# Logit sums in four 32-column groups of TensorE, with the softmax in (slot, head) by token, in a four-layer attention and state-space kernel

## Chip, cores and metric

The kernel runs on one core of a Trainium2 chip. The metric is the device time of one execution in microseconds (us), the median of several runs. Engines: PE is TensorE (PEld its weight loads), DVE is VectorE, ACT is ScalarE, POOL is GpSimd, SP is SyncE, whose queue issues the DMAs. PSUM is the memory that PE writes.

## Reference

The input x is 2048 tokens by 512 features, bfloat16. Four layers follow, A, B, A, B, each of them `x = x + layer(layernorm(x))`, with the same weights in both A and in both B. Layer A, which the change touches, is attention over a dilated window:

```python
H = 32; Dh = D // H            # 32 heads of 16
W, dil = 8, 2                  # 8 keys per token: itself and those 2, 4, ... 14 tokens before
idx = pos[:, None] - off[None, :]
mask = idx >= 0
logits = jnp.einsum("bhsd,bhswd->bhsw", q, kg) * scale
logits = jnp.where(mask[None, None, :, :], logits, -1e9)
attn = _softmax(logits, axis=-1)
o = jnp.einsum("bhsw,bhswd->bhsd", attn, vg)
```

q, k and v come from `x @ wqkv`, and `o @ wo` is what is added to x. Layer B is a long convolution (a state-space kernel), done as a Fourier transform by matmuls; the change leaves it alone.

## The kernel before

Token t sits at partition t // 16 and slot t % 16, so that a slot is a set of 128 tokens, one per partition. Four slots make a block q; there are four blocks. q and k are held transposed (feature by token; four feature tiles `ft` of 128 features, which is 8 heads each), v as token by feature, for 16 slots and 14 slots before them that hold the same rows moved by one partition (`v_ext`, filled by DMA, lines 356 and 357).

Layer A runs in two stretches, in `core` (line 307). In the first, for each block q and feature tile ft:

- `mult` (line 295, DVE) multiplies q with the eight shifted k into the tile prod, 128 features by (8 window positions, 4 slots, 128 tokens). prod has two buffers.
- `lsum` (line 302, PE) sums each head's 16 features. prod is the stationary operand, 128x128 for each window position and slot, and the moving operand is `ind8`, an indicator of 8 columns, one for each of the 8 heads. That is 32 matmuls. The result L (128 tokens by (slot, window, head), float32) fills two PSUM banks; L has two buffers.
- After the last ft, `mask` (line 285, PE) adds -1e9 on partition 0 for positions before the first token.

In the slots of the next block follow `mx` (line 365, DVE maximum over the window), `sub_exp` (line 372, PE subtracts the maximum from L by a matmul with the negative identity; line 375, ACT exponential into ex), `recip` (line 382, PE sums over the window; lines 384 and 386, ACT logarithm and exponential for the reciprocal rs) and `norm_p` (line 392, DVE, attn = ex times rs). Between these stand the projections `q_proj` (line 185) and `v_proj` (line 351) on PE, evacuated by ACT (lines 187 and 353) from two PSUM buffers pq.

In the second stretch, for each slot n in the order 0, 2, 1, 3, 4 ... 15: `pv_mult` (line 402, DVE) multiplies attn with the eight shifted v into pav (two buffers), `pv_sum` (line 412, PE) sums over the window and transposes into po (one buffer), ACT copies it to oT (line 415), and `out_proj` (lines 422 and 424, PE) of the slot before adds x and the projection; ACT writes x back (lines 428 and 430) and takes the layer norm sums (line 108). Blocks 2 and 3 of the softmax, and the products and sums of block 3, lie in this stretch too. In layer 0 ACT also computes sine tables there (line 700) and copies the convolution kernel (line 1354).

The order of all this on PE, DVE, ACT and SP is fixed by the order in which the program calls the functions, inside `tc.manual_schedule`; POOL is left to the scheduler. Before, the order came from loops in `core` with conditions on n and a count `per` that spread the projections; work of other layers came in through a table of events `ev`. The first three products of layer 0 and their sums are called earlier, from `k_gen` (ORDERK, letters X and Z), and share `mult` and `lsum`.

Of the kernel before, what the change touches and what calls it, by code (L numbers as in the profile page):

```python
# [20 lines left out]
P = 128  # L21
# [45 lines left out]

def build_a_consts(tc, nc, cpool, tpool):
# [14 lines left out]
    ind8 = cpool.tile([P, 8], BF16, name="ind8")  # L83
    nc.vector.tensor_tensor(ind8[:], m1[:], m2[:], ALU.mult)
    c["ind8"] = ind8
    rows = cpool.tile([1, P], BF16, name="rows")
    nc.vector.memset(rows[:], 0.0)
    nc.vector.memset(rows[:, 0:1], 1.0)
    c["e0"] = rows[:]
    mv = tpool.tile([1, NA, W], I32, name="iota_mask")  # L90
    nc.gpsimd.iota(mv[:], pattern=[[1, NA], [-2, W]], base=0, channel_multiplier=0)
    mrow = cpool.tile([1, NA, W], BF16, name="maskrow")
    nc.vector.tensor_scalar(mrow[:], mv[:], 0, -1e9, ALU.is_lt, ALU.mult)
    c["maskrow"] = mrow
    c["zrow"] = rows[:, 64:128]
# [67 lines left out]
class LayerA:  # L163
# [110 lines left out]
    def linit(self, q):  # L274
        if "L" in self.st[q]:
            return
        self.st[q]["L"] = self.ps_l.tile([P, 4, W, H], F32, name="L")

    def mask(self, q):
        L = self.st[q]["L"]  # L280
        for j in range(2):
            a = q * 4 + 2 * j
            w0 = a // 2 + 1
            if w0 < W:
                self.nc.tensor.matmul(L[:, 2 * j:2 * j + 2, w0:], lhsT=self.c["e0"],
                                      rhs=self.c["maskrow"][:, a:a + 2, w0:].unsqueeze(3).to_broadcast([1, 2, W - w0, H]),
                                      start=False, stop=True, skip_group_check=True)
# [10 lines left out]
    def lsum(self, q, ft):  # L298
        pr, L = self.st[q].pop(ft), self.st[q]["L"]
        for w in range(W):  # L300
            for al in range(4):
                self.nc.tensor.matmul(L[:, al, w, ft * 8:(ft + 1) * 8], lhsT=pr[:, w, al, :], rhs=self.c["ind8"][:],  # L302
                                      start=(ft == 0 and w == 0 and al % 2 == 0), stop=True, skip_group_check=True)
        if ft == NDT - 1:
            self.mask(q)

    def core(self, x_sb, u, lnp, ev=None, nprod=0):
# [5 lines left out]
        ev = ev or {}  # L313
# [3 lines left out]

        def event(key):
            for f in ev.get(key, ()):
                f()  # L320

        with ExitStack() as c2:
# [25 lines left out]
            def v_proj(a):  # L348
# [5 lines left out]
                if a >= 14:  # L354
# [5 lines left out]
                    event(("v", b))  # L360

            def mx(q):
                L = st[q]["L"]
                m = wk.tile([P, 4, H], BF16, name="mx", bufs=1)
                nc.vector.tensor_reduce(m[:], L[:].rearrange("p a w h -> p a h w"), AX.X, ALU.max)
                st[q]["mx"] = m

            def sub_exp(q):
                L, m = st[q]["L"], st[q]["mx"]
                ex = wk.tile([P, 4, W, H], BF16, name="ex", bufs=1)  # L370
                for j in range(2):
                    nc.tensor.matmul(L[:, 2 * j:2 * j + 2], lhsT=nident[:],
                                     rhs=m[:, 2 * j:2 * j + 2].unsqueeze(2).to_broadcast([P, 2, W, H]),
# [4 lines left out]
            def recip(q):  # L378
                ex, L = st[q]["ex"], st[q]["L"]
                tot = L[:, 0, 0:4, :]  # L380
                for w in range(W):
                    nc.tensor.matmul(tot, lhsT=ident[:], rhs=ex[:, :, w, :], start=(w == 0), stop=(w == W - 1), skip_group_check=True)
                ssum = wk.tile([P, 4, 1, H], F32, name="ssum")
                nc.scalar.activation(ssum[:, :, 0, :], tot, ACT.Ln)
                rs = wk.tile([P, 4, 1, H], BF16, name="rs", bufs=1)
# [3 lines left out]
            def norm_p(q):  # L389
                ex, rs = st[q]["ex"], st[q]["rs"]  # L390
                attn = wk.tile([P, 4, W, H], BF16, name="attn", bufs=2)
                nc.vector.tensor_tensor(attn[:], ex[:], rs[:].to_broadcast([P, 4, W, H]), ALU.mult)
# [4 lines left out]
            def pv_mult(n):  # L397
# [4 lines left out]
                nc.vector.tensor_tensor(pv[:], attn[:, n % 4].unsqueeze(2).to_broadcast([P, W, DH, H]), vap, ALU.mult)  # L402
# [57 lines left out]
            projs = [(q_proj, 1, ft) for ft in range(NDT)] if 1 not in self.qT else []  # L460
            vs = [*range(0, NA, 2), *range(1, NA, 2)]
            projs += [(v_proj, a) for a in vs[:6]] + [(q_proj, 2, ft) for ft in range(NDT)]
            projs += [(v_proj, a) for a in vs[6:]]
            slots = [(0, ft) for ft in range(nprod, NDT)] + [(q, ft) for q in (1, 2) for ft in range(NDT)]
            free = 2 if l else 0
            lead = 0 if l else 2
            per, acc = (len(projs) - lead) / (len(slots) - free - 0.5), float(lead)

            def proj(n):
                nonlocal acc  # L470
                acc += n
                while acc >= 1 and projs:
                    f, *args = projs.pop(0)
                    f(*args)
                    acc -= 1

            for q, ft in slots:
                if q == 1 and ft == 0 and 1 not in self.qT:
                    while 1 not in self.qT or projs[0][0] is q_proj:
# [1000 lines left out]
```

## Time and profile before

| | us |
|---|---|
| median of 3 runs | 422.05 |
| lowest, highest | 421.33, 422.5 |
| the profiled execution, its own time | 418.89 |
| its span in the profile | 417.1 |

In that execution layer 0's logits and projections run from about 104 to 140 us, its weighted sums over v from 140 to 196; in layer 1 from 276 to 312 and from 312 to 364.

| group | count | mean ns |
|---|---|---|
| line 402 DVE products with v | 32 | 2283 |
| line 295 DVE products q with k | 29 + 3 | 2299, 2281 |
| line 302 PE logit sums, 128x8 | 928 + 96 | 166 each, pipelined |
| line 285 PE mask | 14 | 197 to 358 |
| line 365 DVE maximum | 8 | 1218 |
| line 375 ACT exponential | 8 | 1026 |
| line 392 DVE normalization | 8 | 693 |

Timeline rows give start, duration, engine, line, operation, output and input tile with shapes; a number in brackets is the time for which the engine sat idle before the row, with the instruction that ended the wait. A stretch's row gives from:to, its length, and for each engine the busy time with the count of instructions. Matmuls overlap, so that a matmul's duration is its latency, and the spacing of starts is what a stream costs.

### The profile page before, as it was taken

How to read it: one execution, taken by the hardware profiler on the slowest of the kernel's cores; microseconds unless marked ns; L12 is line 12 of the kernel's file. 1: busy time of each engine (PE TensorE's matmuls, PEld its weight loads, DVE VectorE, ACT ScalarE, POOL GpSimd, SP SyncE). 2: the span in 40 equal slices, each digit the busy share in tenths (PEclk: the TensorE clock that was granted, in tenths of full speed). 3: DMA queues.
4: the chain of work that ended last, by engine and by line, in shares of the span. 5: the costliest groups of instructions: out<-in, count | busy, mean ns of one | idle time of the engine just before them, and what ended most of it. 6: DMA issues, size and time to landing. Idle time of an engine off the chain costs nothing.

```text
span 417.1 us, 15864 instructions
## 1 busy us (share of the span) xinstructions
PE 320.5 (77%) x7048; PEld 231.5 (55%) x7106; DVE 387.9 (93%) x515; ACT 321.7 (77%) x552; POOL 37.7 (9%) x46
## 2 busy tenths in 40 slices
PE   3000068999999987778998779999998978896885
PEld 2000036667756565556887768555665655566774
DVE  8999999999899999996999969979779999989995
ACT  6999998987445569987999998863555758779972
POOL 3000200000396000000500000000000020000000
PEclk9999998999999999999999999999999999999899
DMA  8940642113014666393226597730043027504506
GB/s 222 383 125 13 73 90 71 33 40 89 14 40 123 179 180 189 99 389 109 70 89 229 217 306 218 231 99 2 3 114 89 5 79 328 156 3 140 168 10 197
DMA packets 62462, 54.36 MB, mean 130 GB/s; under 512 B 33877, under 2 KB 50874, under 8 KB 61114
## 3 DMA queue, kind: packets, MB, share of 16 engines
q1 hardware_dynamic: 62250, 53.22, 42.0%
q8 instruction: 55, 0.90, 0.9%
q10 hardware_dynamic: 144, 0.13, 0.1%
q14 instruction: 13, 0.11, 0.1%
HBM read 30.28 MB, written 13.24 MB: 104 GB/s over the span
## 4 chain that ended last, share of the span: by engine, by line
PE 35%; DVE 21%; ACT 14%; issue 5%; DMA 5%; SPq 3%; DVEq 0%; ACTq 0%
PE pq L351 6%; DVE pav L402 5%; DVE t L805 5%; PE L L302 4%; DVE a1s L745 4%; PE pk L1175 4%; PE pq L185 3%; DVE prod L295 3%; PE pp L242 3%; PE po L412 3%; PE pp L1113 3%; PE pq L424 2%; SPq L1280 2%; DMA w_sb<-w_dram 2%; ACT ub L818 1%
## 5 line engine op out<-in xcount | busy, mean ns | idle before, releaser
L402 DVE TENSOR_TENSOR pav<-attn,v_ext 128x4096 bf16<-128x4096 bf16 x32 | 72.8, 2283 | 0.1
L295 DVE TENSOR_TENSOR prod<-qT,kT_ext 128x4096 bf16<-128x4096 bf16 x29 | 66.0, 2299 | 3.9 <-PE L L302 3.8
L412 PE MATMUL po<-ident,pav 64*128 64x64 bf16 x2048 | 36.3, 190 | 15.1 <-DVE pav L402 7.7
L412 PEld LDWEIGHTS <-pav 64*128 64x128 bf16 x2048 | 32.5, 95 | 26.0 <-DVE pav L402 14.9
L1103 PE MATMUL pt<-ident,x_blk 128*128 128x128 bf16 x64 | 7.0, 260 | 43.4 <-ACT x_blk L158 43.4
L1015 DVE TENSOR_TENSOR A_t<-A_t,pow_t 128x1024 bf16<-128x1024 bf16 (+4 forms) x46 | 38.1, 868 | 0.2
L424 PE MATMUL pq<-wop,oT 128*128 128x512 bf16 x121 | 31.7, 379 | 4.3 <-issue 3.8
L353 ACT CAST v_ext<-pq 128x512 bf16<-128x512 f32 x32 | 18.8, 587 | 19.2 <-PE pq L351 17.5
L818 ACT CAST ub<-pb 128x1024 bf16<-128x1024 f32 x32 | 32.2, 1036 | 1.7 <-DVE t L805 0.8
L763 PE MATMUL pb<-a1s,w_sb 128*128 128x64 bf16 x768 | 28.4, 196 | 6.2 <-ACT a1s L745 2.9
L302 PEld LDWEIGHTS <-prod 128*128 128x128 bf16 x928 | 27.0, 96 | 8.1 <-DVE prod L295 2.5
L1103 PEld LDWEIGHTS <-x_blk 128*128 128x128 bf16 x64 | 5.4, 117 | 46.1 <-ACT x_blk L158 44.4
L745 DVE CAST a1s<-pb 128x1024 bf16<-128x1024 f32 x23 | 27.0, 1215 | 3.9 <-PE pb L756 3.9
L763 PEld LDWEIGHTS <-w_sb 128*128 128x128 bf16 x768 | 25.8, 100 | 8.6 <-issue 6.8
L351 PE MATMUL pq<-wv,xnT 128*128 128x512 bf16 x118 | 29.9, 379 | 0.5
L1113 PE MATMUL pp<-xnT,kT_ext 128*128 128x512 bf16 x87 | 25.0, 406 | 6.2 <-ACT qT L1118 3.3
L302 PE MATMUL L<-ind,prod 128*128 128x8 bf16 x928 | 27.4, 166 | 0.8 <-DVE prod L295 0.6
L415 ACT CAST oT<-po 128x512 bf16<-128x512 f32 x32 | 18.5, 577 | 11.5 <-PE po L412 11.2
L745 ACT CAST a1s<-pb 128x1024 bf16<-128x1024 f32 x25 | 24.9, 1034 | 2.5 <-PE pb L756 2.2
L1175 PEld LDWEIGHTS <-A_t 128*64 128x64 bf16 (+1 forms) x512 | 22.3, 105 | 3.6
L1175 PE MATMUL pk<-B_t,A_t 128*64 128x84 bf16 (+1 forms) x512 | 24.1, 203 | 0.1
L832 PE MATMUL pb<-Wp,t 64*128 64x64 bf16 x512 | 19.4, 192 | 5.9 <-ACT ub L818 2.8
(225 smaller groups left out, 809.8 us busy)
## 6 DMA issues: line engine op xcount, KB each, us to landing
w_sb<-w_dram SPq DMA_DIRECT2D x8, 1024.0 KB, 9.4
w_dram<-w_zero SPq DMA_DIRECT2D x1, 4096.0 KB, 14.8
kf_ring<-kf_dram SPq DMA_DIRECT2D x13, 256.0 KB, 3.7
kf_ring<-kf_dram SPq DMA_DIRECT2D x26, 128.0 KB, 3.6
v_ext<-v_ext SPq DMA_DIRECT2D x4, 784.0 KB, 6.2
x_blk<-in_A_x_dram SPq DMA_DIRECT2D x4, 512.0 KB, 4.1
kT_ext<-in_A_wqkv_dram SPq DMA_DIRECT2D x4, 512.0 KB, 10.1
x_sb<-in_A_x_dram SPq DMA_DIRECT2D x4, 512.0 KB, 5.4
```

The costliest lines, as they stand in the source:

```text
L295: nc.vector.tensor_tensor(pr, self.qT[q][:, ft].unsqueeze(1).to_broadcast([P, W, 4, P]), kap, ALU.mult)
L302: self.nc.tensor.matmul(L[:, al, w, ft * 8:(ft + 1) * 8], lhsT=pr[:, w, al, :], rhs=self.c["ind8"][:], start=(ft == 0 and w == 0 and al % ...
L351: nc.tensor.matmul(pp[:], lhsT=xnT[:, dt, a * P:(a + 1) * P], rhs=wv[:, dt, :], start=(dt == 0), stop=(dt == NDT - 1))
L402: nc.vector.tensor_tensor(pv[:], attn[:, n % 4].unsqueeze(2).to_broadcast([P, W, DH, H]), vap, ALU.mult)
L412: nc.tensor.matmul(po[:, h, 0, ft, :], lhsT=pvf[rows, w, ft * P:(ft + 1) * P], rhs=ident[rows, rows], start=(w == 0 and ft == 0), stop=(w ...
L424: nc.tensor.matmul(pw[:], lhsT=oT[:, ftp, :], rhs=self.wo[:, ftp, :], start=False, stop=(ftp == NDT - 1))
L745: (self.nc.scalar.copy if eng == "act" else self.nc.vector.tensor_copy)(dst, src)
L763: nc.tensor.matmul(p2[:, j, :], lhsT=self.w2[:, ec * EC + j, :], rhs=a1s[:, ec * EC + j, :], start=True, stop=True)
L818: nc.scalar.copy(ub[:], p2)
L1015: return lambda: nc.vector.tensor_tensor(*args)
L1113: nc.tensor.matmul(pps[kind, b, ft][:], lhsT=la.wqk[:, dt, c:c + P], rhs=la.xnT[:, dt, b * 512:(b + 1) * 512], start=(dt == 0), stop=(dt = ...
L1175: nc.tensor.matmul(o, lhsT=lhs, rhs=Bt[:, ri, c * CH + ql].rearrange("p b g -> p (b g)"), start=(not half and j % 4 == 0 and ri == 0), sto ...
```

## The change

The roles of the two matmul operands in `lsum` are exchanged. The indicator, now 32 columns wide (one of the four feature tiles' 8 heads filled, the rest zero), is the stationary operand; the products are the moving one, 512 columns at a time (4 window positions by 128 tokens). The four slots of a block go to PSUM partitions 0, 32, 64 and 96. That is 8 matmuls per lsum, and L becomes (slot, head) by (window, token). All four feature tiles add into the same 32 partitions of a slot.

The mask becomes a matmul of 4 rows that picks the slot, and touches token column 0 alone. Maximum, subtraction, exponential, sum and reciprocal do the same in the new layout, without a change of size; the normalization is done in place, in ex. A new step `turn` follows it: 8 PE transposes of 128x128 (one per window position) into the second bank of L, and one ACT copy from there into attn, which now lies as token by (window, slot, head).

The loops of `core` are replaced by two strings, CORE0 and CORE1, one letter per call. Read letter by letter they give the order that the loops gave, with T (turn) added: after the normalization of blocks 0 and 1 at the end of the last slot of the following block, and right after the normalization of block 2 (fifth product with v) and of block 3 (twelfth).

```diff
+CORE0 = """
+0mvvvvlmvvxlemqqlmqqlrmvvlnTmvvxlvemvlmvvlrmvvlnTqPxSePmqSOl1PrSO2Pm3qSOlPnT4SOPm56qSOl7P8ASOPmb
+BSOlPxdwCSeOPaaDSOPraaSOPnTbSOPd9ESOPaaFGSOPaaHSOPbtStO
+"""
+CORE1 = """
+0m1l2ml3mqqlmqqvlmvvxlvemvvlmqqlrmqqvlnTmvvxlvemvvlmvvlrmvvlnTqPxSePmqSOlPrSOPmqSOlPnTSOPmqSOlPS
+OPmbSOlPxdwSeOPaaSOPraaSOPnTbSOPdSOPaaSOPaaSOPbtStdaaaaO
+"""
+ROWS0 = (0, 2, 1, 3, 4, 5, 6, 7, 8, 9, 10, 11, 12, 13, 14, 15)
+ROWS1 = (0, 2, 1, 3, 4, 5, 6, 7, 8, 9, 10, 11, 12, 13, 14, 15)
+VROWS = (*range(0, 16, 2), *range(1, 16, 2))
...
-    ind8 = cpool.tile([P, 8], BF16, name="ind8")
-    nc.vector.tensor_tensor(ind8[:], m1[:], m2[:], ALU.mult)
-    c["ind8"] = ind8
-    rows = cpool.tile([1, P], BF16, name="rows")
-    nc.vector.memset(rows[:], 0.0)
-    nc.vector.memset(rows[:, 0:1], 1.0)
-    c["e0"] = rows[:]
-    mv = tpool.tile([1, NA, W], I32, name="iota_mask")
-    nc.gpsimd.iota(mv[:], pattern=[[1, NA], [-2, W]], base=0, channel_multiplier=0)
-    mrow = cpool.tile([1, NA, W], BF16, name="maskrow")
-    nc.vector.tensor_scalar(mrow[:], mv[:], 0, -1e9, ALU.is_lt, ALU.mult)
-    c["maskrow"] = mrow
-    c["zrow"] = rows[:, 64:128]
+    ind = cpool.tile([P, NDT * H], BF16, name="ind32")
+    nc.gpsimd.memset(ind[:], 0.0)
+    diag = bass.AP(tensor=ind.tensor, offset=ind[:].offset, ap=[list(ind[:].ap[0]), [H + 8, NDT], [1, 8]])
+    nc.vector.tensor_tensor(diag, m1[:].unsqueeze(1).to_broadcast([P, NDT, 8]), m2[:].unsqueeze(1).to_broadcast([P, NDT, 8]), ALU.mult)
+    c["ind"] = ind[:].rearrange("p (t h) -> p t h", t=NDT)
+    zrow = cpool.tile([1, 64], BF16, name="zrow")
+    nc.gpsimd.memset(zrow[:], 0.0)
+    c["zrow"] = zrow[:]
+    sv = tpool.tile([4, 4, H], I32, name="iota_slot")
+    nc.gpsimd.iota(sv[:], pattern=[[-1, 4], [0, H]], base=0, channel_multiplier=1)
+    slot = cpool.tile([4, 4, H], BF16, name="slot_sel")
+    nc.vector.tensor_scalar(slot[:], sv[:], 0, None, ALU.is_equal)
+    c["slot"] = slot[:].rearrange("k a h -> k (a h)")
+    mv = tpool.tile([4, 4, W], I32, name="iota_mask")
+    nc.gpsimd.iota(mv[:], pattern=[[4, 4], [-2, W]], base=0, channel_multiplier=1)
+    keep = cpool.tile([4, 4, W], BF16, name="slot_mask")
+    nc.vector.tensor_scalar(keep[:], mv[:], 0, -1e9, ALU.is_lt, ALU.mult)
+    c["mask"] = keep
...
-        self.st[q]["L"] = self.ps_l.tile([P, 4, W, H], F32, name="L")
+        self.st[q]["L"] = self.ps_l.tile([P, W, P], F32, name="L")
 
     def mask(self, q):
         L = self.st[q]["L"]
         for j in range(2):
-            a = q * 4 + 2 * j
-            w0 = a // 2 + 1
-            if w0 < W:
-                self.nc.tensor.matmul(L[:, 2 * j:2 * j + 2, w0:], lhsT=self.c["e0"],
-                                      rhs=self.c["maskrow"][:, a:a + 2, w0:].unsqueeze(3).to_broadcast([1, 2, W - w0, H]),
-                                      start=False, stop=True, skip_group_check=True)
+            w0, w1 = max(2 * q + 1, 4 * j), 4 * j + 4
+            if w0 < w1:
+                self.nc.tensor.matmul(L[:, w0:w1, 0], lhsT=self.c["slot"], rhs=self.c["mask"][:, q, w0:w1], start=False, stop=True,
+                                      skip_group_check=True)
 
...
     def lsum(self, q, ft):
         pr, L = self.st[q].pop(ft), self.st[q]["L"]
-        for w in range(W):
+        for j in range(2):
             for al in range(4):
-                self.nc.tensor.matmul(L[:, al, w, ft * 8:(ft + 1) * 8], lhsT=pr[:, w, al, :], rhs=self.c["ind8"][:],
-                                      start=(ft == 0 and w == 0 and al % 2 == 0), stop=True, skip_group_check=True)
+                self.nc.tensor.matmul(L[al * H:(al + 1) * H, 4 * j:4 * j + 4, :], lhsT=self.c["ind"][:, ft, :],
+                                      rhs=pr[:, 4 * j:4 * j + 4, al, :], start=(ft == 0), stop=True, skip_group_check=True)
         if ft == NDT - 1:
             self.mask(q)
 
...
             def mx(q):
                 L = st[q]["L"]
-                m = wk.tile([P, 4, H], BF16, name="mx", bufs=1)
-                nc.vector.tensor_reduce(m[:], L[:].rearrange("p a w h -> p a h w"), AX.X, ALU.max)
+                m = wk.tile([P, P], BF16, name="mx", bufs=1)
+                nc.vector.tensor_reduce(m[:], L[:].rearrange("c w p -> c p w"), AX.X, ALU.max)
                 st[q]["mx"] = m
 
             def sub_exp(q):
                 L, m = st[q]["L"], st[q]["mx"]
-                ex = wk.tile([P, 4, W, H], BF16, name="ex", bufs=1)
+                ex = wk.tile([P, W, P], BF16, name="ex", bufs=1)
                 for j in range(2):
-                    nc.tensor.matmul(L[:, 2 * j:2 * j + 2], lhsT=nident[:],
-                                     rhs=m[:, 2 * j:2 * j + 2].unsqueeze(2).to_broadcast([P, 2, W, H]),
+                    nc.tensor.matmul(L[:, 4 * j:4 * j + 4], lhsT=nident[:], rhs=m[:].unsqueeze(1).to_broadcast([P, 4, P]),
                                      start=False, stop=True, skip_group_check=True)
                 nc.scalar.activation(ex[:], L[:], ACT.Exp, scale=scale)
                 st[q]["ex"] = ex
 
             def recip(q):
-                ex, L = st[q]["ex"], st[q]["L"]
-                tot = L[:, 0, 0:4, :]
+                ex, tot = st[q]["ex"], st[q]["L"][:, 0, :]
                 for w in range(W):
-                    nc.tensor.matmul(tot, lhsT=ident[:], rhs=ex[:, :, w, :], start=(w == 0), stop=(w == W - 1), skip_group_check=True)
-                ssum = wk.tile([P, 4, 1, H], F32, name="ssum")
-                nc.scalar.activation(ssum[:, :, 0, :], tot, ACT.Ln)
-                rs = wk.tile([P, 4, 1, H], BF16, name="rs", bufs=1)
+                    nc.tensor.matmul(tot, lhsT=ident[:], rhs=ex[:, w, :], start=(w == 0), stop=(w == W - 1), skip_group_check=True)
+                ssum = wk.tile([P, P], F32, name="ssum")
+                nc.scalar.activation(ssum[:], tot, ACT.Ln)
+                rs = wk.tile([P, P], BF16, name="rs", bufs=1)
                 nc.scalar.activation(rs[:], ssum[:], ACT.Exp, scale=-1.0)
                 st[q]["rs"] = rs
 
             def norm_p(q):
                 ex, rs = st[q]["ex"], st[q]["rs"]
-                attn = wk.tile([P, 4, W, H], BF16, name="attn", bufs=2)
-                nc.vector.tensor_tensor(attn[:], ex[:], rs[:].to_broadcast([P, 4, W, H]), ALU.mult)
+                nc.vector.tensor_tensor(ex[:], ex[:], rs[:].unsqueeze(1).to_broadcast([P, W, P]), ALU.mult)
+
+            def turn(q):
+                ex = st[q]["ex"]
+                pt = st[q]["L"][:, 4:8, :].rearrange("c w p -> c (w p)").bitcast(BF16).rearrange("p (w c) -> p w c", w=W)
+                for w in range(W):
+                    nc.tensor.transpose(pt[:, w, :], ex[:, w, :], ident[:])
+                attn = wk.tile([P, W, 4, H], BF16, name="attn", bufs=2)
+                nc.scalar.copy(attn[:].rearrange("p w a h -> p w (a h)"), pt)
                 st[q]["attn"] = attn
 
...
-                nc.vector.tensor_tensor(pv[:], attn[:, n % 4].unsqueeze(2).to_broadcast([P, W, DH, H]), vap, ALU.mult)
+                nc.vector.tensor_tensor(pv[:], attn[:, :, n % 4, :].unsqueeze(2).to_broadcast([P, W, DH, H]), vap, ALU.mult)
```

In the driver, each letter calls the next of its kind: m `mult`, l `lsum`, q and v the projections, x `mx`, e `sub_exp`, r `recip`, n `norm_p`, T `turn`, P `pv_mult`, S `pv_sum`, O `out_proj`, t, b, d and a layer norm steps; digits, w and capital A to H stand for what came in by events.

```diff
+            for c in "".join(order.split()):
+                if c in ev:
+                    ev[c]()
+                else:
+                    next(ops[c])()
```

## The prediction, before the result was known

> **What bounds the kernel now.** I read the page's part 1 first, then busy time by stretches around the two attention layers, then the timelines of VectorE (DVE), TensorE (PE) and ScalarE (ACT) there.
>
> ```profile
> PE 320.5 (77%) x7048; PEld 231.5 (55%) x7106; DVE 387.9 (93%) x515; ACT 321.7 (77%) x552; POOL 37.7 (9%) x46
> ```
>
> DVE is the fullest engine, but the change removes nothing from it. So I ask where DVE waits for PE. By stretch (us, then PE, PEld, DVE, ACT busy): logits and projections of layer 0, its weighted sums over v, the same two of layer 1.
>
> ```profile
> 117.00:139.80 22.80, 22.31 (x338) 14.15 (x344) 21.71 (x13) 11.60 (x22) 15.05 (x10) 1.00 0.43 111
> 139.80:196.00 56.20, 45.42 (x1290) 30.86 (x1304) 53.22 (x46) 45.93 (x97) 1.02 (x1) 1.00 0.57 182
> 282.00:312.00 30.00, 29.63 (x402) 17.89 (x406) 24.89 (x14) 15.80 (x29) 0.00 (x0) 1.00 0.16 41
> 312.00:364.00 52.00, 43.12 (x1283) 29.70 (x1299) 51.68 (x42) 36.00 (x86) 2.89 (x1) 1.00 0.38 132
> ```
>
> In layer 1's logits PE is full (29.63 of 30.00) and DVE is not (24.89); layer 0's logits are balanced; both sums over v are DVE's alone. What PE saves counts only as DVE's waits, which stand in brackets on its timeline:
>
> ```profile
> 114.87 4.49 DVE L295 TENSOR_TENSOR prod<-qT,kT_ext 128x4096 bf16<-128x4096 bf16 x2 [2.07 <-PE L L302]
> ...
> 127.89 0.73 DVE L392 TENSOR_TENSOR attn<-ex,rs 128x1024 bf16<-128x1024 bf16 x1 [0.37 <-ACT rs L386]
> ...
> 139.30 0.69 DVE L392 TENSOR_TENSOR attn<-ex,rs 128x1024 bf16<-128x1024 bf16 x1 [0.72 <-ACT rs L386]
> ```
> ```profile
> 294.96 2.29 DVE L295 TENSOR_TENSOR prod<-qT,kT_ext 128x4096 bf16<-128x4096 bf16 x1 [0.87 <-PE L L302]
> 298.55 0.69 DVE L392 TENSOR_TENSOR attn<-ex,rs 128x1024 bf16<-128x1024 bf16 x1 [1.29 <-ACT rs L386]
> ...
> 311.69 0.69 DVE L392 TENSOR_TENSOR attn<-ex,rs 128x1024 bf16<-128x1024 bf16 x1 [1.29 <-ACT rs L386]
> ```
>
> With the rows at 288.47 (0.61), 301.61 (0.17) and 308.11 (0.87) layer 1 has 5.10 us of such waits. From 312 to 363 DVE's rows follow one another without an idle bracket, so whatever stalls DVE there is paid in full.
>
> [...] Here two 64-column groups do run together, in full: line 756's pairs start 5 ns apart and the next pair 55 ns later; four groups no run here shows. [...]
>
> ```profile
> 196.36 0.22 PE L756 MATMUL pb<-F1c,k_perm 128*64 128x128 bf16 x1
> 196.36 0.22 PE L756 MATMUL pb<-F1s,k_perm 128*64 128x128 bf16 x1
> 196.41 0.22 PE L756 MATMUL pb<-F1c,k_perm 128*64 128x128 bf16 x1
> ```
>
> **The logit sums.** One lsum was 32 matmuls of 8 columns at a pitch of 25 ns, 0.80 us (rows 123.26 to 124.06). It becomes 8 matmuls of 512 columns in two rounds of four column groups. A 512-column stream takes 0.215 us (8 of line 185 from 121.53 on), so two rounds are 0.43 if four groups run together, plus about 0.03 of stagger. Each lsum now enters and leaves a column mode:
>
> ```profile
> 195.74 0.38 PE L424 MATMUL pq<-wop,oT 128*128 128x512 bf16 x1
> ...
> 196.05 0.24 PE L756 MATMUL pb<-F1c,k_perm 128*64 128x128 bf16 x1
> ```
>
> 0.31 us from start to start where 0.215 is the stream: 0.095 to enter. Leaving, 210.46 to 210.61 with 0.053 of stream, is also 0.095. Sum 0.43 + 0.03 + 0.19 = 0.65 us: **0.15 us saved** per lsum, not the 0.37 that the matmuls alone promise. Bounds: 0.45 (switches hidden) to 1.91 (no concurrency, 8 x 0.215 + 0.19). The mask matmuls shrink from up to 448 columns to four at most: block 0's lsum with mask took 1.34 us (117.22 to 118.56), so its mask 0.54; block 1's 0.42 (128.76 to 129.98). New: two small matmuls and a further switch, 0.13. Saved 0.41 and 0.29.
>
> **Layer 1, logits.** Up to the reciprocal of block 1, whose result DVE awaits at 311.69, PE runs ten lsums after the first bound one: 10 x 0.15 + 0.41 + 0.29 = 2.20 us less. The turn of block 0 stands in PE's order there: 8 transposes at 55 ns (line 231: 16 in 0.89 us) are 0.44 us more. Its wait for the normalization hides: that is done at 299.24, and PE gets to it after the lsum at 300.29 and its mask. Its ACT copy (1.01 us by the row xnT<-pt of line 233, same shape) fits ACT's gaps, 15.80 busy of 30; behind it wait the casts of the next v rows, for which pq has two buffers. Net 2.20 - 0.44 = **-1.8 us** of the 5.10.
>
> **Layer 0, logits.** Three lsums precede the product at 114.87, which waited 2.07 for the last of them: -0.7, a little over 0.15 each because the array leaves another column mode before two of them anyway and because the last one's end comes sooner. Then the waits of 0.37 and 0.72 go: PE saves four lsums and a mask, 1.01, before the first, and in all eight lsums and two masks less a turn, 1.46, before the second, against 1.09 to be had. **-1.8 us**; more DVE cannot give.
>
> **The turn in the sums over v.** The normalization of blocks 2 and 3 used to be followed on DVE by products that read it directly. For block 2 four products lie between. For block 3 nothing lies between but small statistics:
>
> ```profile
> 351.58 0.68 DVE L392 TENSOR_TENSOR attn<-ex,rs 128x1024 bf16<-128x1024 bf16 x1
> ...
> 352.45 2.29 DVE L402 TENSOR_TENSOR pav<-attn,v_ext 128x4096 bf16<-128x4096 bf16 x1
> ```
> ```profile
> 353.37 0.19 ACT L118 ACTIVATE ln_rstd<-ln_veps 128x4 f32<-128x4 f32 x1
> ```
>
> The product at 352.45 must now wait for 8 transposes (from 352.3 to 352.9, PE being idle) and then for ACT, which is busy without a gap until it issues the row at 353.37. The copy takes that place and ends near 354.4; the product starts at 354.5: **2.05 us** of new DVE stall, with all DVE rows behind it. The lower bound is an ACT that is free, 1.6 us; the upper, an ACT a row later, 2.8. On PE the sum of row 11 queues behind the turn, 0.7 us late, which the stall covers. Of the stall 0.25 comes back at the end: the last sum began at 362.36, 0.3 after its product, because ACT and PE lagged, and a lag is caught up while DVE stands. Layer 1 ends at -1.8 + 2.05 - 0.25 = **0.0**.
>
> In layer 0 ACT has the same order but is fuller: from 153.98 to 169.7 it has no gap. Block 2's copy, 1.0 us, lands in this run and pushes the evacuations behind it; the seventh sum (168.48, awaiting ACT), the output projection and the last lsum of block 3 follow on PE, and DVE's maximum at 171.76, which had that lsum done just in time (171.69), waits. The shorter lsum and mask give 0.3 back: **+0.7** (0 to 1.0). Block 3's turn: the normalization ends at 181.24, ACT frees itself at 182.1, some 0.3 later with the backlog, so the product at 181.43 starts 2.0 later. The lag at the end is 0.86 here (product over at 191.89, its sum at 192.75); I let 0.75 be caught up. Layer 0: -1.8 + 0.7 + 2.0 - 0.75 = **+0.15**.
>
> **At no cost**: the maximum, exponential and normalization have the same element counts (only strides differ); attn keeps its size; the broadcast in the products over v changes a stride. The constants at the start add three small POOL operations and take one from DVE; DVE has a bracket of 0.30 at 5.59 (awaiting PE) to hide them; without that cover 0.3 us. No DMA is added or moved; SP waits for the same v rows, which come as much earlier as PE does.
>
> **Sum.** 0.15 + 0.0 = +0.2 us on the profiled 418.89, which is 3.16 below the median of the runs shown; on that median 422.05 + 0.2 = **422.3 us**. What a measurement of this kernel can tell from no change is about 0.3%, 1.3 us.
>
> **Rivals.** *Slower: the four groups are not served in full.* Speaking for it: four moving streams at once are nowhere in this trace[...]. [...] If only pairs run together, an lsum costs 1.08: PE then loses 2.8 - 0.7 + 0.4 = 2.5 in layer 1 where it saved 1.8, and about as much in layer 0: +8, 430. Against it: the 64-column pairs lose nothing. It decides the sign from an lsum of 0.72 us on, since fourteen bound lsums times 0.07 is the missing 1.1.
> *Slower: ACT.* If the turn's copies wait a row longer in both layers and no lag is caught up: +0.75 twice and +1.0, so +2.5: 424.7. For it: ACT's packed stretches; against it: gaps of 0.5 follow both.
> *Faster: the switches hide.* If weights for the next mode load during the stream, an lsum takes near 0.46 and saves 0.34: layer 1 gains 3.7 of its 5.1 in place of 1.8, layer 0 0.5 more: -2.2, 420.1. Against it: line 756 is entered from line 763 with 0.094 each time the array is busy (0.123 from start to start, 0.029 of stream).
>
> **How the numbers follow.** As computed, within 1.3 us: 0.40. Groups not served: 0.22; ACT: 0.14 (slower together 0.36). Switches hide, or the stall is shorter: 0.24. The range reaches from 419.6, a little past the faster case, to 426.4[...]; what lies outside is the pairs case and half of the worst of each.
>
> **What would show it.** Right: lsum's eight matmuls in two bursts of four with starts some 10 ns apart, 0.215 between bursts, 0.6 to 0.7 us from the row before to the row after; DVE's brackets in layer 1's logits down from 5.1 to some 3.3 us; one new bracket of about 2 us ahead of the thirteenth product over v in each layer, ended by ACT's attn copy. Wrong: bursts of two or one; brackets before other products; an ACT copy that takes more than 1.1 us; a move of the span outside the two attention layers.

## The result, and the profile after

The changed kernel took 424.59 us (median of 20 runs, 420.89 to 425.87) and the kernel before, beside it on the same chip, 420.99 (20 runs, 418.12 to 425.27): a ratio of 1.0071, 95% interval 1.0051 to 1.0092, some 3.0 us slower. A second measurement of the same pair gave 1.0057 (1.0035 to 1.0080). The forecast was 422.3, which is 0.2 us more than the 422.05 of the three runs that it started from; started from the 420.99 of the 20 runs it would have been 421.2. The range held the result, its middle did not. The profiled execution took 423.45 us with a span of 421.7, against 418.89 and 417.1 before.

Part 1 of the page of after: PE's weight loads fall by 706 and the matmuls on record by 648 (58 matmul records are missing in the trace of before), DVE's busy time is what it was, ACT has 7.5 us more (eight copies of 1.01).

```profile
PE 322.1 (76%) x6400; PEld 210.5 (50%) x6400; DVE 388.3 (92%) x514; ACT 329.2 (78%) x560; POOL 37.8 (9%) x49
```

Inside the two attention layers nearly everything went as computed. One lsum, in PE's timeline of after, layer 1 (a row is start, duration, engine, line, operation, tiles and shapes, count):

```profile
306.19 0.81 PE L362 MATMUL pq<-wv,xnT 128*128 128x512 bf16 x3
306.93 0.61 PE L318 MATMUL L<-prod,ind 128*32 128x512 bf16 x8
307.48 0.39 PE L362 MATMUL pq<-wv,xnT 128*128 128x512 bf16 x1
```

The merged rows hide the starts; singly they are four at 3 to 4 ns from each other, 216 ns, four more, then 0.31 us to the next projection. The projections before them, one 512-column stream at a time, start 216 ns apart too. From the first start to that projection is 0.55 us, of which 0.43 are the two rounds, 0.096 the switch out and the rest the stagger of the starts; with 0.093 for the switch in, the lsum costs 0.64 us. The forecast had 0.65. So the array serves four column groups in full here: four streams take the 216 ns of one.

DVE's brackets in the logits of layer 1, after:

```profile
298.63 2.29 DVE L311 TENSOR_TENSOR prod<-qT,kT_ext 128x4096 bf16<-128x4096 bf16 x1 [0.26 <-ACT v_ext L364]
302.14 0.69 DVE L401 TENSOR_TENSOR ex<-ex,rs 128x1024 bf16<-128x1024 bf16 x1 [1.22 <-ACT rs L396]
...
311.33 2.29 DVE L311 TENSOR_TENSOR prod<-qT,kT_ext 128x4096 bf16<-128x4096 bf16 x1 [0.76 <-ACT v_ext L364]
314.84 0.69 DVE L401 TENSOR_TENSOR ex<-ex,rs 128x1024 bf16<-128x1024 bf16 x1 [1.22 <-ACT rs L396]
```

They add up to 3.46 us where they were 5.11. Against it stands the turn of block 3, whose wait is the one new bracket of each layer (DVE of after, layer 0 and then layer 1), with the ACT rows that it stood behind in layer 1:

```profile
179.78 0.69 DVE L401 TENSOR_TENSOR ex<-ex,rs 128x1024 bf16<-128x1024 bf16 x1
...
182.26 2.29 DVE L419 TENSOR_TENSOR pav<-attn,v_ext 128x4096 bf16<-128x4096 bf16 x1 [1.52 <-ACT attn L409]
```
```profile
354.73 0.69 DVE L401 TENSOR_TENSOR ex<-ex,rs 128x1024 bf16<-128x1024 bf16 x1
...
357.55 2.29 DVE L419 TENSOR_TENSOR pav<-attn,v_ext 128x4096 bf16<-128x4096 bf16 x1 [1.86 <-ACT attn L409]
```
```profile
355.89 0.63 ACT L126 ACTIVATE ln_junk<-x_sb 128x512 bf16<-128x512 bf16 x1
356.43 0.19 ACT L126 ACTIVATION_READ_ACCUMULATOR ln_junk<-x_sb 128x1 f32 x1
356.52 0.99 ACT L409 COPY attn<-L 128x1024 bf16<-128x1024 bf16 x1
```

Layer 0 also has the predicted delay of the maximum (0.55 at 170.98, awaiting the last lsum). Then the surprise. I cut both spans at DVE rows that both have: the first product of q and k in `core`, the first and the thirteenth product with v, the first cast a1s of the layer B that follows, and the same in layer 1. Lengths in us:

| stretch | before | after | change |
|---|---|---|---|
| start to layer 0's first product | 114.87 | 114.39 | -0.48 |
| to its first product with v | 25.04 | 24.16 | -0.88 |
| to the thirteenth | 41.51 | 43.71 | +2.20 |
| to layer B | 15.31 | 15.38 | +0.07 |
| **layer B of layer 0** | **79.42** | **83.48** | **+4.06** |
| layer 1's logits | 36.15 | 34.32 | -1.83 |
| to the thirteenth product with v | 40.15 | 42.10 | +1.95 |
| to layer B | 17.01 | 16.84 | -0.17 |
| last layer B to the end | 47.65 | 47.29 | -0.36 |

Layer 1's attention is at -0.05, as forecast. Of the 4.56 us by which the spans differ, 4.06 lie in layer B, where the change touches nothing and every engine has the same instructions in the same order. DVE of after there:

```profile
243.78 0.69 DVE L771 TENSOR_TENSOR t<-ub,w_sb 128x1024 bf16<-128x1024 bf16 x1 [1.84 <-DMA w_sb<-kn]
...
247.65 1.23 DVE L711 CAST z<-pb 128x1024 bf16<-128x1024 f32 x1 [1.84 <-PE pb L798]
251.30 1.23 DVE L827 TENSOR_TENSOR x_sb<-pb,x_sb 128x1024 bf16<-128x1024 f32 x1 [2.42 <-PE pb L824]
...
259.80 1.41 DVE L131 BATCH_NORM_STATS2 ln_bn<-x_sb 128x6 f32<-128x256 bf16 x4 [1.31 <-ACT x_sb L829]
```

The first wait was not there before (the row at 242.57 follows its predecessor at once), the second was 1.18, the last was not there. The same two rows of before:

```profile
242.57 0.69 DVE L805 TENSOR_TENSOR t<-ub,w_sb 128x1024 bf16<-128x1024 bf16 x1
244.43 1.22 DVE L745 CAST z<-pb 128x1024 bf16<-128x1024 f32 x1 [1.18 <-PE pb L832]
```

The first wait is the largest part of the 4.06 us, and it is a wait for a transfer. PE stood for 2.27 us behind it, and its clock (the third figure from the end of a stretch's row) is then down to 0.51 and 0.64 (one half from 246.0 to 249.4 us), where before has 1.00 in the same two stretches; the longer second wait goes with that:

```profile
246.00:248.00 2.00, 2.00 (x84) 2.00 (x82) 0.35 (x1) 1.01 (x1) 0.35 (x1) 0.51 1.04 379
248.00:250.00 2.00, 2.00 (x84) 1.94 (x79) 0.88 (x1) 1.50 (x2) 0.00 (x0) 0.64 1.02 367
```

Behind the last wait stands PE, which stopped in the middle of a run of equal matmuls:

```profile
255.96 0.27 PE L823 MATMUL pb<-z,g_sb 128*128 128x256 bf16 x1
257.80 0.27 PE L824 MATMUL pb<-z,g_sb 128*128 128x256 bf16 x1 [1.56 <-issue]
```

"issue" means that nothing which the profile shows held it: no semaphore, no buffer.

### The profile page after: what moved, and what is told of

It is laid out like the page before. It is cut to its first block, busy times and chain, and to the rows that moved or that the text cites. A ratio compares the mean times of both kernels' runs of the same rounds, so it can differ in the third digit from the quotient of the medians.

```text
span 421.7 us, 14525 instructions
## 1 busy us (share of the span) xinstructions
PE 322.1 (76%) x6400; PEld 210.5 (50%) x6400; DVE 388.3 (92%) x514; ACT 329.2 (78%) x560; POOL 37.8 (9%) x49
## 3 DMA queue, kind: packets, MB, share of 16 engines
q1 hardware_dynamic: 62250, 53.22, 41.9%
## 4 chain that ended last, share of the span: by engine, by line
PE 34%; DVE 27%; ACT 14%; issue 6%; DMA 4%; SPq 0%; DVEq 0%; ACTq 0%
DVE pav L419 8%; DVE prod L311 6%; DVE a1s L711 4%; PE pk L1141 4%; DVE t L771 4%; PE pq L362 4%; PE pp L1079 3%; PE pp L260 3%; PE po L429 2%; PE pq L203 2%; PE pb L798 2%; PE pq L441 2%; PE L L318 2%; PE pb L729 2%; ACT ln_junk L126 2%
## 5 line engine op out<-in xcount | busy, mean ns | idle before, releaser
L1069 PE MATMUL pt<-ident,x_blk 128*128 128x128 bf16 x64 | 7.0, 260 | 43.4 <-DMA w_dram<-w_q 41.9
L441 PE MATMUL pq<-wop,oT 128*128 128x512 bf16 x128 | 32.8, 379 | 0.0
L729 PE MATMUL pb<-a1s,w_sb 128*128 128x64 bf16 x768 | 27.3, 193 | 6.0 <-ACT a1s L711 2.9
L362 PE MATMUL pq<-wv,xnT 128*128 128x512 bf16 x128 | 30.8, 380 | 0.3 <-ACT kgs L1149 0.3
L1079 PE MATMUL pp<-xnT,kT_ext 128*128 128x512 bf16 x96 | 26.5, 404 | 5.3 <-ACT qT L1084 3.3
L711 DVE CAST a1s<-pb 128x1024 bf16<-128x1024 f32 x23 | 27.1, 1218 | 3.5 <-PE pb L722 3.5
L729 PEld LDWEIGHTS <-w_sb 128*128 128x128 bf16 x768 | 24.8, 98 | 8.4 <-issue 6.5
L798 PEld LDWEIGHTS <-t 64*128 64x128 bf16 x1024 | 18.4, 99 | 12.0 <-issue 7.0
L203 PE MATMUL pq<-xnT,kT_ext 128*128 128x512 bf16 x96 | 23.5, 379 | 0.0
```

The source lines that it names most:

```text
L362: nc.tensor.matmul(pp[:], lhsT=xnT[:, dt, a * P:(a + 1) * P], rhs=wv[:, dt, :], start=(dt == 0), stop=(dt == NDT - 1))
L441: nc.tensor.matmul(pw[:], lhsT=oT[:, ftp, :], rhs=self.wo[:, ftp, :], start=False, stop=(ftp == NDT - 1))
L711: (self.nc.scalar.copy if eng == "act" else self.nc.vector.tensor_copy)(dst, src)
L729: nc.tensor.matmul(p2[:, j, :], lhsT=self.w2[:, ec * EC + j, :], rhs=a1s[:, ec * EC + j, :], start=True, stop=True)
L798: nc.tensor.matmul(p3[:, h, j, :], lhsT=tt[rows, dql, :], rhs=w[rows].rearrange("p m d -> p (m d)"), start=first, stop=not first)
L1079: nc.tensor.matmul(pps[kind, b, ft][:], lhsT=la.wqk[:, dt, c:c + P], rhs=la.xnT[:, dt, b * 512:(b + 1) * 512], start=(dt == 0), stop=(dt = ...
```

## The experiments

Theories at the start: the turn costs more than computed (ACT, or PE's order); the sums save less; or layer B's 4 us have nothing to do with how the attention is computed. Four runs first.

**The same kernel again** (no edit).

> The changed kernel once more, unchanged, for a second profile. In the first profile the two attention stretches together moved by about +0.9 us, as the working said (0.2), and the stretch of layer B between them by +4.0 us (79.4 to 83.5 us from its first a1s copy to layer 1's first product). Theory 1, the extra time there is not tied to the change (waits for DMA landings and a lower TensorE clock in that one execution): here that stretch is again anywhere from 79.5 to 84 us, and profiles of other kernels scatter alike. Theory 2, the change delays layer B in some way: it is 82 to 84 us here and in every kernel with the new sums.

Measured: ratio 1.0057 (1.0035 to 1.0080), span 424.4. Layer B took 82.66 us, again longer than the 79.42 of before, which fits both theories; but layer 0 from its first product with v to layer B now took 61.42 where the first profile had 59.09. The same program loses its microseconds in other places from one execution to the next.

**The sums without the turn, the turn without the sums.** In the first, the normalization writes attn and the transposition is left out:

```diff
-                nc.vector.tensor_tensor(ex[:], ex[:], rs[:].unsqueeze(1).to_broadcast([P, W, P]), ALU.mult)
+                attn = wk.tile([P, W, 4, H], BF16, name="attn", bufs=2)
+                nc.vector.tensor_tensor(attn[:].rearrange("p w a h -> p w (a h)"), ex[:], rs[:].unsqueeze(1).to_broadcast([P, W, P]), ALU.mult)
+                st[q]["attn"] = attn
...
             def turn(q):
...
+                pass
```

> The changed kernel without the turn: no transposes and no copy; the normalization writes attn itself, which therefore lies (slot, head) by token, so this kernel leaves the transposition out of the computation. It shows what the new logit sums alone are worth. Theory 1: DVE's waits shrink by 1.5 us in layer 0 and 2.2 us in layer 1 and nothing is given back, so 3.5 to 4 us less than before outside layer B, ratio 0.991. Theory 2, the new sums or constants cost time in layer B: that stretch is again 82 to 84 us here, and the ratio is 1.000.

In the second, sums, mask and layout are the old ones, and the eight 128x128 pieces of the normalized softmax are turned and copied as in the changed kernel; attn then holds another order than the products with v expect:

```diff
+            def turn(q):
+                ex = st[q]["ex"][:].rearrange("p a w h -> p (a w h)").rearrange("p (k c) -> p k c", k=W)
...
+                for w in range(W):
+                    nc.tensor.transpose(pt[:, w, :], ex[:, w, :], ident[:])
+                attn = wk.tile([P, W, 4, H], BF16, name="attn", bufs=2)
+                nc.scalar.copy(attn[:].rearrange("p w a h -> p w (a h)"), pt)
```

> The logit sums, mask and layout of before, with the turn added behind each normalization (it transposes 128x128 pieces of ex, so attn is a wrong transposition: the layout of attn is changed, nothing else). Theory 1: the turn alone costs 1.5 to 2 us at the thirteenth product in each layer, 0.5 at the maximum of layer 0 and 0.4 of PE in each logit stretch: 4 to 5 us, ratio 1.010. Theory 2: layer B also lengthens by 3 us here only if the turn is what delays it.

Measured: sums alone 416.61 (ratio 0.9877, 0.9833 to 0.9922), turn alone 428.05 (1.0150, 1.0099 to 1.0200). Both signs are as forecast, and both sizes larger (0.991 and 1.010 were expected). The stretch in which neither late transfers nor PE's stops occur, layer 1's logits, prices both cleanly: 36.15 before, 33.88 with the sums alone, 36.60 with the turn alone, 34.32 with both. The sums save 2.27 us there (the forecast: 2.20) and the turn costs 0.44 and 0.45 (the forecast: 0.44). That the sums save less is out. But layer B of layer 0 took 81.40 and 81.41 us, in one kernel with the new sums and in one with the old.

**The turn of block 3 one product earlier.** Its reciprocal moves from the eleventh slot of the second stretch to the tenth, and normalization and turn from the twelfth to the eleventh (layer 1's string; layer 0's alike):

```diff
-OPmbSOlPxdwSeOPaaSOPraaSOPnTbSOPdSOPaaSOPaaSOPbtStdaaaaO
+OPmbSOlPxdwSeOPraaSOPnTaaSOPbSOPdSOPaaSOPaaSOPbtStdaaaaO
```

> The changed kernel with the reciprocal, normalization and turn of block 3 one product with v earlier in both layers. Theory 1, the waits ahead of the thirteenth product (1.52 and 1.86 us) lie on the path: both brackets go, and the span of each layer's sums over v is 1.3 to 1.9 us shorter; ratio to the kernel before about 1.000. Rival: ACT, which is nearly full there, moves its wait to another product, and less than 0.5 us comes back.

Measured: 422.51 (ratio 1.0022, 0.9995 to 1.0048). The bracket before the thirteenth product is gone in both layers; layer 1's way to that product is 40.15 us, exactly that of before (0.87 us of this gain was lost again on the way to its layer B, 17.71 us for 16.84). Yet layer 0 gained nothing: from its first product with v to layer B it took 61.30. There PE stopped again:

```profile
182.94 1.08 PE L429 MATMUL po<-ident,pav 64*128 64x64 bf16 x62
186.96 0.24 PE L429 MATMUL po<-ident,pav 64*128 64x64 bf16 x2 [2.94 <-issue]
```

The stretches of 2 us show what goes with it (columns: from:to, length, busy time of PE, PEld, DVE, ACT and POOL with counts, PE's clock, share of the DMA engines, GB/s):

```profile
182.00:184.00 2.00, 2.00 (x67) 1.26 (x66) 2.00 (x4) 1.66 (x6) 0.00 (x0) 1.00 1.00 418
184.00:186.00 2.00, 0.02 (x2) 0.00 (x0) 1.71 (x3) 1.42 (x3) 0.00 (x0) 1.00 1.00 406
186.00:188.00 2.00, 1.04 (x5) 0.43 (x5) 0.77 (x1) 0.58 (x1) 0.00 (x0) 0.59 0.33 135
188.00:190.00 2.00, 2.00 (x28) 0.89 (x28) 2.00 (x3) 0.52 (x2) 0.00 (x0) 0.50 0.08 25
190.00:192.00 2.00, 2.00 (x50) 1.39 (x45) 0.88 (x2) 1.97 (x6) 0.00 (x0) 0.50 0.00 0
```

The DMA engines are full at 406 to 418 GB/s while PE stands; they empty, PE starts, and its clock is then one half for nearly 7 us (0.59, 0.50 and 0.50 in the rows above, 0.70 in the next 2 us). Here the stop was 2.94 us. Stops of 1.57 us (turn alone) and 1.78 us (the kernel before with 32 idle transposes, below) were followed by some 3 us of a slower PE: in the first the clock is 0.65 and 0.78 in the two stretches of 3 us from 189 us on, in the second four matmuls that take 1.03 us elsewhere took 1.55. Stops of 1.04 and 1.56 us in after left the clock at 1.00. So in these profiles the slower clock does not follow from the stop alone; what sets it is not shown.

**What PE was waiting for.** Part 3 of after's page has a queue of the kind "instruction":

```profile
q8 instruction: 50, 0.82, 0.9%
```

50 packets for 12,800 matmuls and weight loads are 256 for each; in the kernel before 55 for 14,212 (twice its 7,106 weight loads), 258. In both profiles all its packets have one size, 16,384 bytes. My reading of these counts is that PE's program comes in pieces of 256 by DMA. I counted PE's instructions ahead of each stop of over 0.4 us that ends in "issue" (two for each weight load and its matmul, one for each that only waits): after 100 us there are 37 such stops in the fourteen profiles of this study, and at every one the count, divided by 256, leaves 193 or 194. So the stops lie whole pieces of 256 apart, and I take these places as the borders of the pieces.

Every one of the fourteen profiles has as many packets of q8 as borders, so the two can be paired in order. Each of the 37 stops then ended 1.2 to 1.8 us after the landing of the packet of the border before, and at none of the 671 borders after 100 us did PE go on sooner than 1.1 us after that landing. That fits a packet which starts at one border and brings what PE needs at the next. It takes 1.1 us (median). Where the DMA engines are less than half busy in the 2 us behind a border (371 of the 671), it starts 1.7 us after the border at the latest; where they are over 95% busy (103), 2.9 us after it (median), and up to 5.3. In after it starts 2.9, 4.2, 4.2 and 3.0 us behind the borders at 181.1, 250.8, 257.8 and 350.3 us, where the DMA share of the next 2 us is 1.03, 0.92, 1.22 and 0.99. The second of these landed at 256.1 us; PE came to the next border at 256.2 and went on at 257.8. From 200 to 241 us the packets of after start 3.7 to 5.7 us apart, which is what a piece lasts at PE's pace there; a delay of 4.2 us uses up most of that.

That gives the third theory a mechanism: on this reading the change takes instructions out of PE's program, so the borders fall on other work. It can be tried without touching anything else, since PE idles for 41.9 us at the start:

```profile
50.12 0.29 PE L1069 MATMUL pt<-ident,x_blk 128*128 128x128 bf16 x1 [41.88 <-DMA w_dram<-w_q]
```

**Idle transposes in that gap**, in the kernel before, in the changed one and in the one with the early turn, so many that all borders move by a quarter, a half or three quarters of a piece (32, 64 or 96 transposes, each with a weight load):

```diff
             pt = xps[b, d] = la.ps_tr.tile([P, 2, 4, P], BF16, name="pt")
+            if (b, d) == (0, 0):
+                for k in range(64):
+                    nc.tensor.transpose(pt[:, 0, 0, :], ident[:], ident[:])
```

In what was written ahead of these runs, theory A is the third theory with its mechanism; B and C are its rivals.

> The changed kernel with 64 more transposes of the identity at the start, 128 TensorE instructions that lie in its idle stretch of 42 us before the first transposition of x; nothing reads them. Theory A (instruction supply): TensorE's queue stops without a releaser only where 193 is left when the instruction's number is divided by 256, which is a piece of 256 instructions that arrives late; it arrives late where transfers fill the DMA engines (about 175-187 us, 249-260 us and 350-358 us). Then the added instructions move the stops to other work by half a piece, the remainder 193 stays, and the median moves by 1 to 3 us in one direction or the other from 424.2. Theory B (dependencies alone set the time): idle time is filled with idle work, so the median stays at 424.2 within 0.6 and layer 0 from its first product over v to layer B takes the 59.1 to 61.4 us that it took.

> The kernel before with the same 64 transposes in the same idle stretch. Theory A: the kernel before meets late pieces too (0.83 and 0.92 us at 182 and 188 us in its profile), in a favourable place; moved by half a piece it should lose 1 to 3 us: a median of 422.5 to 424.5, with layer 0 from the first product over v to layer B longer than 56.8 us or layer B longer than 79.4 us. Theory B: 421.5 within 0.6, and layer B of layer 0 again at 79.4 us.

> The version with block 3's turn ahead of two more sums, with 32 more transposes of the identity in the idle stretch (64 TensorE instructions). Without the pad: 422.5, of which a stop of 2.94 us at 187 us and a TensorE clock of one half for some 6 us after it. Theory A: the stop moves by a quarter of a piece; 418.5 if it comes to lie in a wait, 424 if not. Theory B: 422.5 within 0.6.

> The same with 64 transposes, half a piece. Theory A: the stop at 187 us goes to other work; without it and its slow clock the attention of layer 0 should end 3 us earlier: 419.5; in an unfavourable place 424. Theory B: 422.5 within 0.6.

> The changed kernel with 32 idle transposes in the idle stretch at the start (64 TensorE instructions, a quarter of a piece). Theory A (instruction supply decides where the pieces' borders fall on the work): again a median of its own between 419.5 and 425, no stop without a releaser at another remainder than 193. Mean of the changed kernel over its four places (0, 64, 128, 192): within 1.5 us of that of the kernel before, since the mean takes the luck of the place out and leaves the change itself, computed at +0.2. Rival C (the change itself costs 3 us, the 128 pad merely found a hole): this run at 424 or more and the mean 2 us or more above that of before.

> The same with 96 idle transposes, three quarters of a piece. Theory A: a median between 419.5 and 425. Rival C: 424 or more.

> The kernel before with 32 idle transposes. Theory A: between 420 and 425, so that the mean over the four places lies near 422.7, above the unpadded 421. Rival C: 421 to 421.5, with 424.5 of the half-piece pad the exception.

> The kernel before with 96 idle transposes. Theory A: between 420 and 425. Rival C: 421 to 421.5.

Measured, median in us and ratio to the kernel before without idle transposes, with its interval:

| idle transposes | kernel before | changed kernel | early turn |
|---|---|---|---|
| 0 | 420.88 to 421.59, 1 | 424.59, 1.0071; 423.92, 1.0057 | 422.51, 1.0022 (0.9995-1.0048) |
| 32 | 426.05, 1.0123 (1.0089-1.0156) | 419.96, 0.9981 (0.9960-1.0002) | 419.53, 0.9947 (0.9922-0.9973) |
| 64 | 424.50, 1.0114 (1.0074-1.0153) | 420.49, 1.0012 (0.9984-1.0040) | 419.59, 0.9979 (0.9958-1.0000) |
| 96 | 422.66, 1.0040 (1.0018-1.0062) | 420.15, 0.9983 (0.9960-1.0006) | not run |
| mean | 1.0069 | 1.0010 | 0.9983 |

Work that nothing reads, in time that nothing uses, moves the kernel before by up to +1.2% and the changed kernel by -0.5 to -0.8%. Theory B and rival C of these expectations fall: all three padded versions of the changed kernel are below 421, all three of the kernel before above 422. Some of my own numbers missed: before with 32 came to 426.05, above the 425 named; the changed kernel with 64 moved by 3.7 us where 1 to 3 were named; the early turn with 32 came to 419.53, between the 418.5 and the 424 named; and the means differ by 0.0059 (2.5 us), more than the 1.5 us allowed. The early turn's mean is over three places, not four. The transposes do nothing else that I can see: layer 0's first product in `core` stands at 114.1 to 114.9 us in all profiles of the three kernels, padded or not, though the clock is recorded lower in the idle gap itself: 0.50 from 18 to 60 us with 64 of them in the changed kernel, 1.00 from 8 to 50 us without.

In the padded profile with 64, layer B of layer 0 is back at 79.38 us. Its DVE rows, to be held against those of after above (none with w_sb, 1.18 before z, none before the last statistics):

```profile
241.94 0.69 DVE L771 TENSOR_TENSOR t<-ub,w_sb 128x1024 bf16<-128x1024 bf16 x1
243.81 1.22 DVE L711 CAST z<-pb 128x1024 bf16<-128x1024 f32 x1 [1.18 <-PE pb L798]
247.23 1.23 DVE L827 TENSOR_TENSOR x_sb<-pb,x_sb 128x1024 bf16<-128x1024 f32 x1 [2.20 <-PE pb L824]
...
254.81 1.35 DVE L131 BATCH_NORM_STATS2 ln_bn<-x_sb 128x6 f32<-128x256 bf16 x4
```

With 96 it took 79.36. With 32 it took 83.65: there the border fell on the end of a run that DVE waits for, and PE stood for 2.54 us.

```profile
250.54 0.19 PE L798 MATMUL pb<-Wp,t 64*128 64x64 bf16 x1
253.27 0.19 PE L798 MATMUL pb<-Wp,t 64*128 64x64 bf16 x1 [2.54 <-issue]
```

The same stretch in the kernel before took 79.42 without idle transposes and 84.63, 81.08 and 80.19 with 32, 64 and 96. Over the four places its mean is 81.33 before and 81.47 after: the +4.06 us of the first comparison was the best place of one kernel against a bad place of the other, in one execution of each.

**An observation beside it.** The wait for w_sb in after is a late transfer, not a stop of PE. Seven of the fourteen profiles have it (0.36 to 1.84 us), the others not. In layer B of layer 0 (issued from 203 to 238.5 us) the fourteen profiles have 250 transfers of 128 or 256 KB with a landing on record. Where no packet of q8 runs between 0.8 and 1.9 us after the issue they take 2.09 us (median of 116; 1.96 to 2.55 from the tenth to the ninetieth per cent), where one does 3.32 us (134; 2.07 to 4.02). So with a piece on its way data landed some 1.2 us later. This was seen and not varied by itself.

## Why the prediction came out as it did

**The logit sums** (0.65 us, 0.15 saved): right, 0.64. The rival in which four groups are not served in full is dead, and so is that of the hidden switches, at 0.093 and 0.096 each. How long two rounds take where four groups are served in part, no run shows.

**Layer 1, logits** (-1.8): right, -1.83, and in its parts 2.27 and 0.44.

**Layer 0, logits** (-1.8 up to the first product with v): -1.36. The brackets of 0.37 and 0.72 went, as computed; the 0.7 of the first product came to 0.48, and what remained of the 1.09 came to 0.88.

**The turn of block 3** (2.05 and 2.0): 1.86 and 1.52, behind the ACT rows named. The copy took the place that the working gave it, ahead of the row ln_rstd; in layer 0 the backlog of 0.3 on ACT did not come. With the lag caught up at the end (0.25 forecast, 0.17 measured) layer 1 is at -0.05 against 0.0. **Block 2's turn** (+0.7): the maximum waits 0.55, and the way to it is 0.58 longer. Layer 0's lag (0.75 to be caught up) was not caught up in the unpadded profiles (15.31 to 15.38, and 17.49 in the second) and was in the padded ones (14.17 to 14.18 in all three). In the unpadded two PE stood there for 1.04 and 2.09 us, in the padded ones for 0.92 at most. So the step was right where PE was not stopped for longer.

**Where it failed: "At no cost", and with it the sum.** The range held 424.59 by its width and not by its reasons: 3.0 us more than before stand against the +0.2 of the sum, more than the 1.3 us named for the case as computed. "At no cost" asked what the removed and added instructions cost on the engines and in DMAs that the program issues, and found that no DMA is added or moved. On the engines it held: the maximum takes 1218 ns before and after, the exponential 1026, the normalization 693 and 687, a product with v 2283 and 2284. But q8 has 50 packets where it had 55, and with some 1,400 matmuls and weight loads taken out (14,212 to 12,800) the borders fall on other work. What had been set to zero came, in these two executions, as +4.06 us in layer B: the last wait of 1.31 us stands behind a stop at a border, the first of 1.84 is the late transfer of w_sb, with the slower clock behind it. Both waits were gone with 64 and with 96 idle transposes; by what way the place of the borders makes the transfer late is not shown. The forecast had named "a move of the span outside the two attention layers" as a sign against it, and that is what came. None of the rivals had it: the one for +2.5 us (ACT's copies wait longer) ends at nearly the measured time, and is not what happened, since both new brackets were shorter than computed and not longer. The faster rival's time is 0.2 us too high, since its -2.2 holds the +0.2 already (419.9), and fourteen times 0.07 us is 0.98 and not 1.1; nothing here rests on these.

**What the change itself is worth** with the place taken out: the mean ratio goes from 1.0069 to 1.0010 over four places each, -2.5 us; the four profiles' mean spans from 421.44 to 419.78, -1.7. From place to place a ratio varies by 0.59% (before) and 0.39% (after, its two unpadded ones taken as one), so the mean difference of 0.59% has a standard error of about 0.35%. The forecast of +0.2 us (0.05%) is within two of these, and four of the 128 places do not settle the sign. For the same reason the 416.61 and 428.05 of the two part changes, each in one place, show the direction and not the size.

**A version ahead of both**: the early turn with 32 idle transposes, 419.53, ratio 0.9947 to the kernel before. Its profile still has 83.91 us in layer B and a stop of 2.90 us there; a place without it was not looked for.

## What to carry to other kernels

A change of some tenths of a per cent to a program with thousands of matmuls has to be measured at several places of its instruction stream, both versions alike: idle transposes in an early gap cost nothing here and moved all borders. Read a bracket that ends in "issue" together with the DMA share of the same two microseconds and with the count of PE's instructions ahead of it: equal remainders of 256 (193 or 194 at all 37 stops here) went with late packets of q8, and not with the code that stands there. And a handover from DVE through PE and ACT back to DVE can be priced by rows well (1.86 and 1.52 us here for 2.0), and is best placed with other products between: with one product with v between, the bracket was gone in both layers.

## What the hardware showed that I had not expected

- All 37 stops of PE over 0.4 us that end in "issue" (after 100 us, fourteen profiles) stand where the count of its matmuls, weight loads and waits leaves 193 or 194 when divided by 256, and q8 has one packet for each place in the count with that remainder. The packet takes 1.1 us (median). It starts at most 1.7 us after its border with the DMA engines less than half busy, and 2.9 us after it (median; up to 5.3) with them over 95% busy. PE went on at no border sooner than 1.1 us after the landing of the packet before, and stood for 0.4 to 2.9 us where that was late.
- The longest of these stops (2.94 us) was followed by nearly 7 us at half of PE's clock, two of 1.57 and 1.78 us by some 3 us of a slower PE, and one of 1.56 us by none.
- Four moving streams of 512 columns into four column groups started 3 to 4 ns apart and took 216 ns together, as one such stream does; a change between this form and outputs of 128 columns cost 0.093 to 0.096 us.
- One program's own runs spread over up to 1.6% (420.71 to 427.63 us in one set), and its two profiles differ in where the time goes (59.09 and 61.42 us in layer 0 from the first product with v to layer B, 83.48 and 82.66 in layer B). What sets that was not tried.
